# Two tables for a planner that orders an attention and two MLPs on one core

## The chip, the core and the metric

One core of a Trainium2 chip runs the whole program in one launch. TensorE multiplies matrices, VectorE, ScalarE and GpSimd work elementwise, SyncE (SP) issues the transfers. The metric is device microseconds of one execution. The kernel before takes 909.75 us, median of 3 runs (909.4 to 910.39).

## The reference

```python
a = softmax(phi, axis=2)                       # per batch and head, over the sequence
k_m, v_m = einsum('bhsm,bhsd->bhmd', a, k), einsum('bhsm,bhsd->bhmd', a, v)
attn = softmax(q @ k_m.T / sqrt(64)) @ v_m     # 4 batches, 8 heads, 576 tokens, 64 wide, 32 memories
x = attn as (2304, 512)
h = x @ w_in; x = (h * sigmoid(1.702 * h)) @ w_out            # 512 -> 2048 -> 512
xn = x / sqrt(mean(x * x) + 1e-6) * rms_g
out = (silu(xn @ w_gate) * (xn @ w_val)) @ w_out2             # 512 -> 1536 -> 512
```

All inputs are float32; some weights arrive as 64-bit floats, read as pairs of 32-bit words.

## The kernel before, in words

Products run as split pairs: each operand is a rounded part (h) and a remainder (l), and each product is three products, hh, hl and lh. So every converted weight, and every intermediate, needs a rounding copy (mostly ScalarE) and a subtraction for the remainder (sub_lo, GpSimd or VectorE).

The steps are small functions. For each unit u = (batch, group of four heads) the attention goes from ld_phi and ld_src (loads) through att_k1t or att_k1, att_k2 to att_k5 (the memories) and att_q1, att_q3, att_q3s, att_q4 (the queries). The first MLP works on pairs of batches, pr = 0 and 1, and in 8 groups g of 256 hidden columns; vm_part multiplies the values by w_in, a_g1 (pr, g, t) makes gelu for a quarter t of the tokens, a_g2 multiplies by w_out and adds into x2. norm_1 to norm_4 scale. The second MLP is b_g3 (gate, value, their product) and b_g4 (w_out2, added into oacc, and the transfer out), in 6 groups and 6 tiles of 384 tokens. w_load brings half a weight tile, w_conv makes 32-bit floats of it: ScalarE's absolute value, then on VectorE a clamp (tensor_scalar with max and min, lines 549 to 552), a shift and mask, and two bit operations, then a rounding copy and the remainder (line 579). The converted first-MLP weights are written to a cache in DRAM and read back for the second pair.

All of these only record operations. The class Plan then orders them: units (an operation, or a run of products into one PSUM tile) have a duration from `cost` (line 179), a due time from `dues` (line 255), and `order` (line 295) simulates the engines; wherever an engine can start several units within a small slack it takes the one whose due time is earliest. Due times run from the first to the last product and are pulled forward through the predecessors:

```python
u.due = t if u.eng == "PE" and u.line else t + self.LAG
for s in u.then:
    u.due = min(u.due, s.due + s.after[u] - res if u in s.after else s.due)
```

`can` (line 278) says from when a unit's buffers are free: a tag is a ring of slots, and units that aren't urgent leave `spare` slots. `Pulse` (line 39) models TensorE's two clock rates, and `fill` (line 374) puts products of ones_r by itself into the planned gaps of TensorE. `locks` (line 212) keeps VectorE operations with two operands in SBUF, and its fast ones, from overlapping with GpSimd in the plan. At the end `issue` hands every operation to its engine in the planned order (line 403, which is why nearly every instruction of the trace has line 403). Engines work through their queues in that order.

Of the kernel before, what the change touches and what calls it, by code (L numbers as in the profile page):

```python
# [38 lines left out]
class Pulse:  # L39
# [8 lines left out]
    def rate(self, t):  # L48
        k = int(t / self.W)
        if k not in self.slow:  # L50
            j = max(self.slow)
            while j < k:
                share = self.busy.get(j, 0.0) / self.W
                self.slow[j + 1] = share < (0.93 if self.slow[j] else 0.5)
                j += 1
        return 2.0 if self.slow[k] else 1.0

    def took(self, t, occ, dry=False):
        took = left = occ * self.rate(t)
        while not dry and left > 1e-9:  # L60
            k = int(t / self.W)
            part = min(left, (k + 1) * self.W - t + 1e-6)
            self.busy[k] = self.busy.get(k, 0.0) + part
            t, left = t + part, left - part
        return took

# [27 lines left out]
class Tag:  # L94
    def __init__(self, n, strict, spare, ahead):
        self.strict, self.spare, self.ahead = strict, spare, ahead
        self.free, self.queue, self.line, self.next = [0.0] * n, [], [], 0


class Held:  # L100
    def __init__(self, tag, ap):
        self.tag, self.ap, self.users, self.place = tag, ap, [], None


class Unit:
# [11 lines left out]
class Plan:  # L117
# [6 lines left out]
    LAG = 20.0  # L124
    FILL = True

    def __init__(self, nc):
        self.real = dict(zip(self.ENGINES, (nc.gpsimd, nc.tensor, nc.vector, nc.scalar, nc.sync)))
        self.ops, self.tiles, self.seen, self.line, self.keen = [], {}, {}, False, False
        for name in self.ENGINES:  # L130
            setattr(self, name, Queue(self, name))

# [10 lines left out]
        return sum(1 << i for i in range(4) if p0 < 32 * i + 32 and p0 + rows > 32 * i), m  # L143

    def add(self, op):
        self.ops.append(op)
        for x, write in [(x, False) for x in op.ins] + [(op.out, True)]:
            name = x.tensor.name
            held = self.tiles.get(name)
            if held:  # L150
                if x.space == bass.MemoryType.PSUM:

                    q, m, write = 15, 1, True
                else:
                    q, m = self.area(x)
                if held.users:
                    op.behind.append(held.users[0])
                else:
                    op.takes.append(held)
                    held.place = len(held.tag.queue)  # L160
                    held.tag.queue.append(held)
                    held.line, held.rank = op.line, len(held.tag.line)
                    if op.line:
                        held.tag.line.append(held)
                held.users.append(op)
                op.uses.append(held)
            elif name.startswith("cache"):
                q, m = 1, 1 << x.offset // 65536
            else:
                continue  # L170
            past = self.seen.setdefault(name, [])
            op.after += [o for o, oq, om, w in past if (w or write) and oq & q and om & m]
            if write:
                past[:] = [y for y in past if y[1] & ~q or y[2] & ~m]
            past.append((op, q, m, write))


    @staticmethod
    def cost(op):
        def size(x):  # L180
            return reduce(int.__mul__, (n for s, n in x.ap[1:]), 1)

        n = size(op.out)
        if op.eng == "PE":
            if op.name == "transpose":
                return 0.0009 * n, 0.0009 * n + 0.16
            if op.kw["lhsT"].dtype == F32R:
                t = 0.0135 + n / 2400
                return t, t + 0.16
            t = 0.05 if size(op.kw["lhsT"]) == 32 else 0.1 if n > 1 else 0.13  # L190
            return t, t + 0.25
        if op.eng == "ACT":
            return 0.08 + n / 1200, 0.18 + n / 1200
        if op.eng == "POOL":
            two = op.name == "tensor_tensor"
            t = 0.15 + 0.00215 * n if two else 0.05 + 0.00104 * n
            return t, t + 0.05
        if op.eng == "DVE":
            rate = 1920 if Plan.fast(op) else 960
            if op.name == "tensor_reduce":  # L200
                n, rate = size(op.ins[0]), 960 if op.ins[0].ap[-1][0] == 1 else 560
            t = 0.075 + n / rate + (0.04 if n < 20 else 0.0)
            return t, t + 0.08
        return 0.47, 0.0

    @staticmethod
    def fast(op):
# [10 lines left out]
    def units(self):  # L218
# [27 lines left out]
            for p in [*u.after, *u.behind]:  # L246
                p.then.append(u)
        for held in self.tiles.values():
            held.users = list(dict.fromkeys(of[o] for o in held.users))
            held.left = len(held.users)  # L250
        for u in units:
            u.uses = list(dict.fromkeys(h for o in u.ops for h in o.uses))
        return units

    def dues(self, units):

        t = 0.0
        for u in units:
            u.due = t if u.eng == "PE" and u.line else t + self.LAG
            if u.eng == "PE":  # L260
                t += u.occ
        for u in reversed(units):
            dma = 4.0 if u.eng == "SP" else 0.0
            res = u.res + dma + self.SEM
            for s in u.then:
                u.due = min(u.due, s.due + s.after[u] - res if u in s.after else s.due)
            for h in u.uses:
                queue = h.tag.queue if h.tag.strict else h.tag.line
                j = (h.place if h.tag.strict else h.rank) + h.tag.ahead
                if j < len(queue) and (h.tag.strict or h.line):  # L270
                    s = queue[j].users[0]
                    if s.k > u.k:
                        u.due = min(u.due, s.due - res)
            for h in u.takes:
                if h.tag.strict and h.place + 1 < len(h.tag.queue):
                    u.due = min(u.due, h.tag.queue[h.place + 1].users[0].due)

    def can(self, u):

        t = 0.0  # L280
        for h in u.takes:
            tag = h.tag
            if tag.strict and tag.next != h.place:
                return None
            if len(tag.free) <= (0 if u.keen else tag.spare):
                return None
            if u.eng == "PE" and not u.line and any(
                p.start is None and p not in h.users
                for c in h.users if c.eng != "PE" for p in c.after
            ):  # L290
                return None
            t = max(t, sorted(tag.free)[0 if u.keen else tag.spare])
        return t

    def order(self):
        units = self.units()
        self.dues(units)
        free = dict.fromkeys(self.ENGINES, 0.8)
# [6 lines left out]
        while got < len(units):  # L305
# [20 lines left out]
            if best is None:  # L326
                raise RuntimeError(self.stuck(ready))
            t, u = best
            e = u.eng
            ready[e].remove(u)  # L330
            got += 1
            u.bound = (free[e], u.ready, self.can(u), lock if u.locks else 0.0)
            if e == "PE":
                fill = self.fill(u, free[e], t, pulse) if self.FILL else []
                fills += fill
                took = pulse.took(t, u.occ)
                u.start, u.done, free[e] = t, t + took + u.res - u.occ, t + took
            else:
                u.start, u.done, free[e] = t, t + u.res, t + u.occ
# [10 lines left out]
            for h in u.takes:  # L350
                tag = h.tag
                tag.next = max(tag.next, h.place + 1)
                at = max(x for x in tag.free if x <= t + 1e-9)
                tag.free.remove(at)
            for h in u.uses:
                h.left -= 1
                if not h.left:
# [1 line left out]
            for s in u.then:  # L359
                s.wait -= 1  # L360
                if u in s.behind:
                    s.ready = max(s.ready, u.start)
                elif s.eng != e or e == "SP":
                    s.ready = max(s.ready, u.done + self.SEM - s.after[u])
                if not s.wait:
# [8 lines left out]
    def fill(self, u, free, t, pulse):  # L374

        held = next((h for h in u.takes), None)
        if held is None:
            return []
        ops, at, t = [], max([free, min(x for x in held.tag.free)]), t - 0.3
        while True:  # L380
            took = pulse.took(at, 0.0135 + 512 / 2400, dry=True)
            if at + took > t:
# [24 lines left out]
def kernel(  # L407
# [663 lines left out]
    for o in range(4):  # L1071
        nc.vector.memset(maskeo[32 * o : 32 * o + 32, o % 2 : o % 2 + 1], 1.0)

    def line(step, *args):
        plan.line = True
        step(*args)
        plan.line = False

    def do(step):
        plan.keen = step[0] in (norm_1, norm_2, norm_3, norm_4)  # L1080
        step[0](*step[1:])
        plan.keen = False

    def conv(hf):
        w_conv(hf)

    def att_steps(u, k3, k3s, q1, q3s):
        if u[0] < 2:
# [24 lines left out]
            yield from [(norm_4, pr, t, e) for e in range(NE)]  # L1113

    def weights(hf):
        w_load(hf)
        conv(hf)

    def unit(u, k3, q3s):
# [24 lines left out]

    def loads(b):
        for g in range(2):
            ld_phi((b, g))
            ld_src((b, g), 0)
            ld_src((b, g), 1)

    loads(0)
    ins, outs = halves(groups[0])[:2], halves(groups[0])[2:]
    for hf in ins:
        w_load(hf)
    for g in range(2):
        ld_src((0, g), 2)
    for hf in ins:
        conv(hf)
    for g in range(2):
# [4 lines left out]
        line(vm_part, 0, 0, c, 0)  # L1164
    loads(1)
    for g in range(2):
        ld_src((1, g), 2)
    SP.dma_start(out=rg, in_=moe2_rms_g.rearrange("(e p) -> p e", p=P))

    side, per, prev = iter(()), 2, None  # L1170
# [72 lines left out]
```

## Time and profile before

| | us |
|---|---|
| median of 3 runs | 909.75 |
| the profiled execution | 907.28 |
| its span | 905.5 |
| TensorE busy | 887.7 (98%) |
| VectorE busy | 534.4 (59%) |
| ScalarE busy | 412.0 (45%) |
| GpSimd busy | 311.4 (34%) |

The ends of products are modelled in the trace, so a busy TensorE is not one at its peak; products of ones_r count as busy too. Names of tiles come without their number: gr is a_g1's output and its remainder, x is x2, stage the attention's tile, pad and cv the tiles in which weights are converted, a_inh and a_inl a weight's rounded part and remainder. POOL is GpSimd, DVE VectorE, ACT ScalarE, PE TensorE, SPq the queue of SP.

### The profile page before, as it was taken

The numbers are of one execution on the slowest core, as the hardware profiler recorded it, in microseconds if no ns is written. First come the engines' busy times: TensorE is split into PE (matmuls) and PEld (weight loads), VectorE is DVE, ScalarE is ACT, GpSimd is POOL, SyncE is SP. The second block draws the span as 40 slices with busy tenths as digits, with TensorE's granted clock in tenths as the row PEclk, the third lists the DMA queues.
The fourth block names the chain that finished last, engine by engine and source line by source line (L and its number), as shares of the span: only waits on it lengthen the run. The fifth ranks groups of instructions, "written<-read, shape, count | busy, mean of one in ns | idle before, by whom it ended". The sixth has DMA issues, their size and how long they took to land.

```text
span 905.5 us, 15206 instructions
## 1 busy us (share of the span) xinstructions
PE 887.7 (98%) x5916; PEld 841.6 (93%) x5916; DVE 534.4 (59%) x1059; ACT 412.0 (45%) x895; POOL 311.4 (34%) x316
## 2 busy tenths in 40 slices
PE   8999999999999999999999999999999999999997
PEld 6889999888989999999999999999999999999997
DVE  3765888779855355758886574375356337333333
ACT  2665866775757755646656451132132132112110
POOL 1244555544678768775650030021021021001000
PEclk8999999999999999999999999999999999999999
DMA  9961747638321112123332022022003000000124
GB/s 237 243 188 62 195 141 186 176 115 240 97 83 35 49 35 59 54 65 118 93 94 71 1 73 68 1 70 70 1 24 116 1 1 24 1 1 1 51 54 105
DMA packets 40536, 74.64 MB, mean 82 GB/s; under 512 B 3856, under 2 KB 16144, under 8 KB 40464
## 3 DMA queue, kind: packets, MB, share of 16 engines
q1 hardware_dynamic: 40464, 73.68, 29.0%
q8 instruction: 46, 0.75, 0.4%
q14 instruction: 26, 0.21, 0.1%
HBM read 60.56 MB, written 13.11 MB: 81 GB/s over the span
## 4 chain that ended last, share of the span: by engine, by line
PE 81%; DVE 5%; ACT 5%; DMA 4%; POOL 3%; issue 2%; SPq 0%; POOLq 0%; ACTq 0%; DVEq 0%
PE pg L403 74%; DMA raw_a_in<-in_moe_w_in_dram 3%; DVE pad L403 2%; PE pk L403 2%; PE pq L403 2%; PE pvm L403 1%; DMA stage<-in_v_dram 1%; POOL gr L403 1%; ACT L403 1%; ACT pad L403 1%; PE pk4s L403 1%; DVE x L403 1%; ACT gf L403 0%; POOL a_outl L403 0%; DVE stage L403 0%
## 5 line engine op out<-in xcount | busy, mean ns | idle before, releaser
L403 PE MATMUL pg<-gr,a_outh 128*128 128x288 f32 x960 | 204.9, 297 | 0.6 <-POOL gr L403 0.6
L403 PEld LDWEIGHTS pg<-gr,a_outh 128*128 128x128 f32 x960 | 157.7, 188 | 1.5 <-POOL gr L403 1.1
L403 PE MATMUL pg<-gr,a_outl 128*128 128x288 f32 x480 | 141.4, 295 | 0.3 <-POOL a_outl L403 0.3
L403 PE MATMUL pg<-b_o2h,pp 128*128 128x512 f32 x432 | 139.5, 391 | 0.3 <-ACT oacc L403 0.3
L403 POOL TENSOR_TENSOR gr<-gf,gr 128x288 fp32r<-128x288 f32 x128 | 107.8, 856 | 87.4 <-ACT gr L403 69.0
L403 DVE TENSOR_TENSOR x<-x,pg 128x288 f32<-128x288 f32 x224 | 95.8, 447 | 68.3 <-PE pg L403 67.4
L403 DVE TENSOR_TENSOR pf<-sg,pg 128x384 f32<-128x384 f32 x72 | 39.8, 552 | 150.8 <-PE pg L403 131.2
L403 POOL TENSOR_TENSOR b_o2l<-cv,b_o2h 128x512 fp32r<-128x512 f32 x12 | 15.4, 1301 | 267.0 <-ACT b_o2h L403 267.0
L403 ACT ACTIVATE sg<-pg 128x384 f32<-128x384 f32 x72 | 35.4, 492 | 156.7 <-PE pg L403 155.7
L403 PEld LDWEIGHTS pg<-b_o2h,pp 128*128 128x128 f32 x432 | 81.1, 188 | 16.6 <-ACT oacc L403 0.4
L403 ACT CAST pp<-pf 128x384 fp32r<-128x384 f32 x72 | 37.0, 514 | 128.0 <-DVE pf L403 127.5
L403 PEld LDWEIGHTS pg<-gr,a_outl 128*128 128x128 f32 x480 | 90.2, 188 | 0.8 <-POOL a_outl L403 0.5
L403 PE MATMUL pg<-b_o2l,pp 128*128 128x512 f32 x216 | 84.7, 392 | 0.0
L403 DVE TENSOR_TENSOR oacc<-oacc,pg 128x512 f32<-128x512 f32 x90 | 61.5, 684 | 31.4 <-PE pg L403 31.3
L403 ACT ACTIVATE gf<-pg 128x288 f32<-128x288 f32 x128 | 51.1, 409 | 42.3 <-PE pg L403 41.1
L403 ACT CAST gr<-gf 128x288 fp32r<-128x288 f32 x128 | 54.1, 435 | 18.3 <-PE pg L403 11.7
L403 PE MATMUL pg<-xnh,b_gateh 128*128 128x384 f32 x288 | 62.1, 337 | 0.0
L403 PE MATMUL pg<-xnh,b_gatel 128*128 128x384 f32 x288 | 61.8, 335 | 0.0
L403 PE MATMUL pg<-xnh,b_valh 128*128 128x384 f32 x288 | 61.7, 335 | 0.0
L403 PE MATMUL pg<-xnh,b_vall 128*128 128x384 f32 x288 | 61.5, 334 | 0.0
L403 PE MATMUL pg<-xnl,b_valh 128*128 128x384 f32 x288 | 61.5, 334 | 0.0
L403 PE MATMUL pg<-xnl,b_gateh 128*128 128x384 f32 x288 | 61.5, 334 | 0.0
(192 smaller groups left out, 1783.2 us busy)
## 6 DMA issues: line engine op xcount, KB each, us to landing
raw_a_in<-in_moe_w_in_dram SPq DMA_DIRECT2D x16, 512.0 KB, 5.2
raw_a_out<-in_moe_w_out_dram SPq DMA_DIRECT2D x16, 512.0 KB, 4.7
cache<-pad SPq DMA_DIRECT2D x32, 256.0 KB, 4.6
raw_b_gate<-in_moe_w_gate_dram SPq DMA_DIRECT2D x12, 512.0 KB, 3.7
raw_b_val<-in_moe_w_val_dram SPq DMA_DIRECT2D x12, 512.0 KB, 3.6
raw_b_o<-in_moe_w_out_dram SPq DMA_DIRECT2D x12, 512.0 KB, 3.6
stage<-in_k_dram SPq DMA_DIRECT2D x8, 576.0 KB, 7.0
stage<-in_v_dram SPq DMA_DIRECT2D x8, 576.0 KB, 10.5
```

The source lines that it names most:

```text
L403: getattr(self.real[op.eng], op.name)(*op.args, **op.kw)
```

## The change

Every step gets a name, its function and its whole numbers (`at`), and every operation its number within the step. Two tables go by these names. OTHER names operations that go to the other one of VectorE and GpSimd: 98 steps, 122 operations. HASTE names 57 steps whose due time is shifted, 47 earlier (4.6 to 67.8 us) and 10 later (0.9 to 96.5 us). Besides, the planner's costs change (products of the attention longer, PSUM operands longer on ScalarE and VectorE, a gap of 0.03 between dependent VectorE operations), its model of the clock (a lower threshold for slowing down, products of few columns count less), and its slots: a unit takes the slot that was released first.

| operations in OTHER | from | to | number |
|---|---|---|---|
| a_g1, remainder (8 and 17), first pair | GpSimd | VectorE | 26 |
| a_g1, remainder, second pair | GpSimd | VectorE | 20 |
| w_conv a 0, clamp (1) | VectorE | GpSimd | 22 |
| w_conv a 0, remainder (7) | GpSimd | VectorE | 15 |
| w_conv a 1, remainder (1) | GpSimd | VectorE | 11 |
| w_conv b, clamp (1) | VectorE | GpSimd | 4 |
| w_conv b, remainder (6) | GpSimd | VectorE | 4 |
| att_k3, subtraction (2) | GpSimd | VectorE | 2 |
| att_q3s, multiplication (3) | GpSimd | VectorE | 5 |
| norm_1, addition of 768 (2) | GpSimd | VectorE | 3 |
| norm_1, remainder (5) | GpSimd | VectorE | 2 |
| norm_4, remainder (2) | VectorE | GpSimd | 7 |
| b_g3 0 0, remainder (27) | VectorE | GpSimd | 1 |

```diff
-                self.slow[j + 1] = share < (0.93 if self.slow[j] else 0.5)
+                self.slow[j + 1] = share < (0.93 if self.slow[j] else 0.36)
...
-    def took(self, t, occ, dry=False):
+    def took(self, t, occ, streams=1.0, dry=False):
...
-            self.busy[k] = self.busy.get(k, 0.0) + part
+            self.busy[k] = self.busy.get(k, 0.0) + part * streams
...
+    HASTE = {
+        "a_g1 0 2 2": 34.2,
...
+        "b_g4 5 4": -96.5,
+        "ld_src 0 0 1": 46.6,
...
+        "w_conv a 0 4 in 1": 40.2,
+        "w_conv a 0 5 out 0": 41.1,
+        "w_conv a 1 7 in 0": 67.8,
...
+        "w_load a 0 4 out 0": 57.5,
+        "w_load b 0 o2 0": 34.1,
+    }
+
+    OTHER = {
+        "a_g1 0 0 1": (8,),
...
+        "norm_4 0 2 2": (2,),
+        "w_conv a 0 0 in 0": (7,),
+        "w_conv a 0 0 in 1": (1, 7),
...
+    }
...
+        k = self.count[self.step] = self.count.get(self.step, -1) + 1
+        op.step = self.step
+        if k in self.OTHER.get(self.step, ()):
+            op.eng = "POOL" if op.eng == "DVE" else "DVE"
...
-            t = 0.05 if size(op.kw["lhsT"]) == 32 else 0.1 if n > 1 else 0.13
+            t = 0.094 if size(op.kw["lhsT"]) == 32 else 0.17 if n > 1 else 0.22
...
-            return 0.08 + n / 1200, 0.18 + n / 1200
+            t = 0.08 + n / 1200
+            if op.ins[0].space == bass.MemoryType.PSUM:
+                t += 0.13 if op.kw.get("func") is AF.Gelu_apprx_sigmoid else 0.07
+            return t, max(t + 0.04, 0.18 + n / 1200)
...
+            if any(x.space == bass.MemoryType.PSUM for x in op.ins):
+                t += 0.04
...
+        return {1: 0.0, 32: 0.7}.get(op.out.ap[-1][1], 1.0)
...
+            u.due -= self.HASTE.get(u.ops[0].step, 0.0)
...
-            t = max(t, sorted(tag.free)[0 if u.keen else tag.spare])
+            t = max(t, tag.free[0])
...
-                at = max(x for x in tag.free if x <= t + 1e-9)
-                tag.free.remove(at)
+                tag.free.pop(0)
...
+                elif s.eng == e == "DVE":
+                    s.ready = max(s.ready, u.done + 0.03)
...
+    def at(step, *args):
+        said = [a for a in args if isinstance(a, (int, tuple))]
+        plan.step = " ".join([step.__name__, *map(str, said)]).replace("(", "").replace(")", "").replace(",", "").replace("'", "")
...
     def do(step):
+        at(*step)
...
     def conv(hf):
+        at(w_conv, hf)
         w_conv(hf)
```

## Rows read from the trace of the kernel before

**Rows 1.** Stages of the span: busy us of each engine (instructions), PEclk, DMA share, GB/s.

```profile
0.00:44.00 44.00, 41.04 (x303) 34.47 (x304) 24.85 (x70) 17.93 (x44) 10.02 (x19) 0.88 0.97 240
44.00:100.00 56.00, 52.22 (x462) 48.08 (x461) 39.48 (x95) 36.52 (x91) 24.56 (x24) 1.00 0.49 130
100.00:275.00 175.00, 169.98 (x1432) 162.82 (x1431) 138.79 (x292) 117.88 (x273) 99.98 (x102) 1.00 0.54 152
275.00:498.00 223.00, 221.77 (x1598) 218.36 (x1597) 144.20 (x284) 139.99 (x298) 142.17 (x147) 1.00 0.22 68
498.00:905.00 407.00, 402.74 (x2129) 377.92 (x2127) 187.06 (x322) 99.68 (x194) 34.67 (x26) 1.00 0.13 37
```

**Rows 2.** Chain of waits, whole span, in order of time: start us, us, what.

```profile
497.74 403.01 PE pg L403 x2130
...
900.77 0.69 DVE oacc L403
```

**Rows 3.** The same stages, TensorE's products with ones_r alone: stretch, PE busy, PEclk, DMA.

```profile
0.00:44.00 44.00, 22.37 (x76) 0.88 0.97 240
...
44.00:100.00 56.00, 10.09 (x41) 1.00 0.49 130
...
100.00:275.00 175.00, 8.73 (x35) 1.00 0.54 152
```

**Rows 4.** Chain of waits between 35 and 190 us.

```profile
35.98 9.03 DMA stage<-in_v_dram
...
89.83 1.03 DVE stage L403 x2
...
155.47 11.49 DMA raw_a_in<-in_moe_w_in_dram
...
177.54 1.61 DVE pad L403 x4
...
180.08 5.70 DMA raw_a_in<-in_moe_w_in_dram
```

**Rows 5.** Stages again, 200 to 250 us.

```profile
200.00:250.00 50.00, 48.65 (x402) 45.85 (x401) 44.02 (x96) 33.20 (x75) 29.47 (x30) 1.00 0.61 168
```

**Rows 6.** Timeline, 27 to 30 us: start us, us, engine, line, operation, count.

```profile
27.79 1.27 POOL L403 TENSOR_TENSOR a_inl<-pad,a_inh 128x512 fp32r<-128x512 f32 x1 [1.99 <-ACT a_inh L403]
...
27.89 1.72 DVE L403 SCALAR_TENSOR_TENSOR pad<-raw_a_out,pad 128x512 uint32<-128x512 uint32 x1
...
29.80 0.68 DVE L403 SCALAR_TENSOR_TENSOR pad<-raw_a_out,pad 128x512 uint32<-128x512 uint32 x1
```

**Rows 7.** Groups by shape: busy us, mean ns | idle before, who ended it.

```profile
L403 POOL TENSOR_TENSOR gr<-gf,gr 128x288 fp32r<-128x288 f32 x128 | 107.8, 856 | 87.4 <-ACT gr L403 69.0 <-PE pg L403 10.2 <-issue 7.7
...
L403 DVE TENSOR_TENSOR x<-x,pg 128x288 f32<-128x288 f32 x224 | 95.8, 447 | 68.3 <-PE pg L403 67.4
...
L403 DVE TENSOR_TENSOR oacc<-oacc,pg 128x512 f32<-128x512 f32 x90 | 61.5, 684 | 31.4 <-PE pg L403 31.3
...
L403 POOL TENSOR_TENSOR a_inl<-raw_a_in,a_inh 128x512 fp32r<-128x512 f32 x16 | 21.0, 1310 | 1.1
...
L403 DVE TENSOR_SCALAR pad<-pad 128x512 f32<-128x512 f32 x32 | 15.5, 484 | 11.1 <-ACT pad L403 11.1
...
L403 DVE TENSOR_TENSOR xnl<-xnf,xnh 128x384 fp32r<-128x384 f32 x24 | 14.0, 593 | 3.4 <-ACT xnh L403 3.3
...
L403 POOL TENSOR_TENSOR stage<-stage 96x384 f32<-96x384 f32 x16 | 13.0, 829 | 26.7 <-DVE stage L403 21.1 <-ACT stage L403 4.2 <-DVE vm_0l L403 1.1
...
L403 POOL TENSOR_SCALAR a_inh<-raw_a_in 128x512 fp32r<-128x512 f32 x16 | 10.2, 638 | 3.6 <-PE pvm L403 2.9 <-DMA raw_a_in<-cache 0.7
...
L403 DVE TENSOR_TENSOR stage<-pq,stage 96x384 f32<-96x384 f32 x16 | 8.7, 551 | 0.4
...
L403 POOL TENSOR_TENSOR sr<-sq,sr 128x384 fp32r<-128x384 f32 x6 | 6.7, 1110 | 4.1 <-ACT sr L403 4.1
```

**Rows 8.** Timeline at 152 us, SP's queue.

```profile
152.21 0.36 SPq L403 DMA_DIRECT2D stage<-in_k_dram  x1
```

More of the change, by code (lines that the diff above doesn't have):

```diff
@@ L96, in __init__ @@
         self.strict, self.spare, self.ahead = strict, spare, ahead
-        self.free, self.queue, self.line, self.next = [0.0] * n, [], [], 0
+        self.n, self.free, self.queue, self.line, self.next = n, [0.0] * n, [], [], 0
 class Held:
     def __init__(self, tag, ap):
-        self.tag, self.ap, self.users, self.place = tag, ap, [], None
+        self.tag, self.ap, self.ops, self.place = tag, ap, [], None
 class Unit:
@@ L125 @@
     FILL = True
+    HASTE = {
+        "a_g1 0 2 2": 34.2,
+        "a_g1 0 3 0": -35.6,
+        "a_g1 0 6 2": 17.9,
+        "a_g1 1 3 2": 57.3,
+        "a_g1 1 3 3": 40.2,
+        "a_g1 1 6 3": 24.6,
+        "a_g1 1 7 0": 28.0,
+        "a_g1 1 7 2": 17.0,
+        "a_g2 0 0 3": 35.8,
+        "a_g2 0 2 3": -19.2,
+        "a_g2 0 3 1": 7.7,
+        "a_g2 1 0 2": 41.3,
+        "a_g2 1 1 1": 41.2,
+        "att_k1 3 0": 35.9,
+        "att_k3 3 0": 20.5,
+        "att_k4 2 1": 32.9,
+        "att_k4 3 0": 7.4,
+        "att_k5 1 0": 58.0,
+        "att_k5 2 0": -36.4,
+        "att_q1 2 0 0": 22.5,
+        "att_q1 2 1 1": 15.0,
+        "att_q3 2 0 0": 20.7,
+        "att_q3 3 0 0": -0.9,
+        "att_q3 3 1 1": 52.4,
+        "att_q3s 2 1 0": -28.4,
+        "att_q3s 2 1 1": 11.8,
+        "att_q3s 3 0 1": 17.9,
+        "att_q4 1 1 0": 54.2,
+        "att_q4 2 0 1": -9.3,
+        "att_q4 3 0 1": -11.3,
+        "b_g3 0 2": 6.4,
+        "b_g3 1 0": 34.5,
+        "b_g3 1 4": -15.0,
+        "b_g3 1 5": 4.6,
+        "b_g4 5 4": -96.5,
+        "ld_src 0 0 1": 46.6,
+        "norm_2 0 2": 23.2,
+        "norm_3 0 1": 22.5,
+        "norm_4 0 0 2": 28.2,
+        "norm_4 0 1 0": -19.0,
+        "norm_4 0 1 3": 5.2,
+        "norm_4 1 1 1": 26.5,
+        "vm_part 0 1 1 0": 19.0,
+        "vm_part 0 3 0": 18.6,
+        "vm_part 0 3 1": 19.5,
+        "vm_part 0 6 0": 29.2,
+        "vm_part 0 7 0": 37.3,
+        "vm_part 0 7 1": 17.5,
+        "vm_part 1 1 0": 41.6,
+        "vm_part 1 3 1": 50.7,
+        "w_conv a 0 4 in 1": 40.2,
+        "w_conv a 0 5 out 0": 41.1,
+        "w_conv a 1 7 in 0": 67.8,
+        "w_conv b 0 o2 0": 20.1,
+        "w_conv b 0 val 0": 28.6,
+        "w_load a 0 4 out 0": 57.5,
+        "w_load b 0 o2 0": 34.1,
+    }
+    OTHER = {
[98 rows of a table added]
+    }
     def __init__(self, nc):
@@ L129, in __init__ @@
         self.ops, self.tiles, self.seen, self.line, self.keen = [], {}, {}, False, False
+        self.step, self.count = "", {}
         for name in self.ENGINES:
@@ L145, in add @@
     def add(self, op):
+        k = self.count[self.step] = self.count.get(self.step, -1) + 1
+        op.step = self.step
+        if k in self.OTHER.get(self.step, ()):
+            op.eng = "POOL" if op.eng == "DVE" else "DVE"
+        op.key = self.step, k
         self.ops.append(op)
@@ L155, in add @@
                     q, m = self.area(x)
-                if held.users:
-                    op.behind.append(held.users[0])
+                if held.ops:
+                    op.behind.append(held.ops[0])
                 else:
@@ L164, in add @@
                         held.tag.line.append(held)
-                held.users.append(op)
+                held.ops.append(op)
                 op.uses.append(held)
@@ L202, in cost, with streams @@
             t = 0.075 + n / rate + (0.04 if n < 20 else 0.0)
+            if any(x.space == bass.MemoryType.PSUM for x in op.ins):
+                t += 0.04
             return t, t + 0.08
         return 0.47, 0.0
+    @staticmethod
+    def streams(op):
+        return {1: 0.0, 32: 0.7}.get(op.out.ap[-1][1], 1.0)
     @staticmethod
@@ L248, in units @@
         for held in self.tiles.values():
-            held.users = list(dict.fromkeys(of[o] for o in held.users))
+            held.users = list(dict.fromkeys(of[o] for o in held.ops))
             held.left = len(held.users)
+            held.tag.free, held.tag.next = [0.0] * held.tag.n, 0
         for u in units:
@@ L291, in can, with order @@
                 return None
-            t = max(t, sorted(tag.free)[0 if u.keen else tag.spare])
+            t = max(t, tag.free[0])
         return t
-    def order(self):
+    def order(self, until=1e9):
         units = self.units()
@@ L328, in order @@
             t, u = best
+            if t > until:
+                self.planned = units
+                return None
             e = u.eng
@@ L335, in order @@
                 fills += fill
-                took = pulse.took(t, u.occ)
+                took = pulse.took(t, u.occ, self.streams(u.ops[-1]))
                 u.start, u.done, free[e] = t, t + took + u.res - u.occ, t + took
@@ L378, in fill @@
             return []
-        ops, at, t = [], max([free, min(x for x in held.tag.free)]), t - 0.3
+        ops, at, t = [], max(free, held.tag.free[0]), t - 0.3
         while True:
@@ L1072 @@
         nc.vector.memset(maskeo[32 * o : 32 * o + 32, o % 2 : o % 2 + 1], 1.0)
+    def at(step, *args):
+        said = [a for a in args if isinstance(a, (int, tuple))]
+        plan.step = " ".join([step.__name__, *map(str, said)]).replace("(", "").replace(")", "").replace(",", "").replace("'", "")
     def line(step, *args):
+        at(step, *args)
         plan.line = True
@@ L1084, in conv, with load @@
     def conv(hf):
+        at(w_conv, hf)
         w_conv(hf)
+    def load(hf):
+        at(w_load, hf)
+        w_load(hf)
     def att_steps(u, k3, k3s, q1, q3s):
@@ L1115, in weights @@
     def weights(hf):
-        w_load(hf)
+        load(hf)
         conv(hf)
@@ L1146, in loads @@
         for g in range(2):
-            ld_phi((b, g))
-            ld_src((b, g), 0)
-            ld_src((b, g), 1)
+            do((ld_phi, (b, g)))
+            do((ld_src, (b, g), 0))
+            do((ld_src, (b, g), 1))
     loads(0)
@@ L1153 @@
     for hf in ins:
-        w_load(hf)
+        load(hf)
     for g in range(2):
-        ld_src((0, g), 2)
+        do((ld_src, (0, g), 2))
     for hf in ins:
@@ L1166 @@
     for g in range(2):
-        ld_src((1, g), 2)
+        do((ld_src, (1, g), 2))
+    plan.step = "rg"
     SP.dma_start(out=rg, in_=moe2_rms_g.rearrange("(e p) -> p e", p=P))
```

94 rows, old and new, of the table OTHER are left out of this document.

## The prediction

> **What bounds the kernel now.** I read the table of stages first, all engines in five stretches [rows 1]. In the last one, 498 to 905 us, TensorE works 402.7 of 407.0 us, and VectorE needs only 187.1 of them. The chain of waits says the same: one piece of 403.0 us with nothing but matrix products, then an addition and the last transfer [rows 2]. No order of the other engines shortens that, so 44% of the span is out of reach.
>
> What can be gained is TensorE's time that is not a product of the program: its idle time (stretch minus busy, [rows 1]) and the filler products that the plan puts into planned gaps; they multiply ones_r by itself [rows 3]. (In the fourth stretch ones_r is the operand of the norm's products, so none is counted there.)
>
> - 0 to 44 us: idle 3.0, filler 22.4. TensorE waits here for the attention of batch 0. DMA is at 0.97 of its time, so I take this stretch as set by the loads.
> - 44 to 100: idle 3.8, filler 10.1, together 13.9.
> - 100 to 275: idle 5.0, filler 8.7, together 13.7.
> - 275 to 498: idle 1.2, no filler.
>
> From 44 us on, 28.8 us are lost, and that is the most that a better order gives back behind the start. The chain names the losers [rows 4]: in 44 to 100 the load of v for batch 1 (9.03 us on the chain) and then VectorE's softmax; in 100 to 275 the weights, a load that lands after 11.49 us, VectorE's four operations per half weight (one piece of 1.61 us is pad alone), then the next load, 5.70 us. VectorE is the fullest engine behind TensorE: 138.8 of 175 us, and 44.0 of 50 between 200 and 250 [rows 1, 5].
>
> **The shared resource.** At 27.79 GpSimd starts a two-input subtraction of 1.27 us; VectorE's operation on pad that begins at 27.89 takes 1.72 us, while the next of the same kind takes 0.68 alone [rows 6]. An operation of VectorE with two operands in SBUF stands still while GpSimd works. So a GpSimd operation costs VectorE too, and I count both engines and the sum of what they hold, called port time below.
>
> **The table of engines, first pair (slots up to about 290 us).** Durations from [rows 7].
>
> - 26 subtractions of a_g1 (128x288) go from GpSimd, 0.856 us each, to VectorE. With both operands in SBUF this shape isn't in the trace. The same shape with one operand in PSUM takes 0.447; the 384 wide one in SBUF takes 0.593, waits included. I take 0.45, nearest in shape. GpSimd -22.3, VectorE +11.7.
> - 15 subtractions of converted weights (128x512): GpSimd 1.310; VectorE 0.69, by the 512 wide addition (0.684). GpSimd -19.7, VectorE +10.4.
> - 22 clamps of the conversion (tensor_scalar, 128x512) go the other way. VectorE gives 0.484 each, -10.6. On GpSimd the trace shows multiply and add in this shape, 0.638; maximum and minimum it doesn't show, so between 0.638 and the two-input 1.310. I take 0.64: GpSimd +14.1. Each adds a hop to another engine behind ScalarE's absolute value, and queues there behind a subtraction of up to 1.31 us.
> - Attention: five multiplications (0.829 against 0.551) and two subtractions of 768 columns. VectorE's additional column costs (0.684-0.447)/224 = 1.06 ns, so 0.551+0.41 = 0.96; GpSimd takes at least twice its 0.829. VectorE +4.7, GpSimd -7.5.
>
> Sum: VectorE +16.2 us, GpSimd -35.4. Port time: -35.4 + 11.7 + 10.4 + 4.7 - 10.6 = -19.2 us. VectorE gets more work but fewer stops; the two nearly cancel, and what is left is latency: the subtractions that end a_g1 and a weight half, which TensorE waits for, take about half as long.
>
> The Trainium skill speaks against the clamps. Its page "VectorE: DVE Perf Modes", section "Mode 2×_2P — use both read ports for one tensor", says that a float tensor_scalar on SBUF data runs at two elements a cycle on VectorE, by using both read ports. By that rule the move trades VectorE's fastest form for one that blocks it 0.64 us: 22 times 0.16 us worse than the 0.484 it frees, 3.5 us of port time lost. The trace agrees that the form is fast [rows 7]. The sum above already holds these 3.5 us.
>
> **The same table later.** In the second pair (to 498) 20 subtractions of a_g1, 11 of weights, and three additions of 768 and two subtractions of the norm go to VectorE, seven subtractions of norm_4 to GpSimd (0.593 against 1.110): VectorE about +9.0+7.6+2.9+1.1-4.2 = +16.4 on 144.2 of 223 us, 72%. TensorE's 221.8 of 223 hide it; I cost it at nothing. Without cover, the seven would add 7 x 0.52 = 3.6 us. In the last stage four clamps, four subtractions and one subtraction of b_g3 lie beside 402.7 us of TensorE: nothing.
>
> **The table of shifts.** 57 steps, 47 earlier and 10 later. It adds no instruction; it changes who goes first where several units can start, and through the dues of predecessors the loads in front of them. A conversion that goes earlier brings its load, its cache write and its place in SP's, ScalarE's, VectorE's and GpSimd's queues with it, and all that is behind waits for it. Where it can pay: the load of 11.49 us, issued at 155.47, stands behind the next unit's k, v and q, whose issues begin at 152.21 [rows 8]; without them it would land nearer to the 3 to 6 us of the next one on the chain (5.70), some 6 us. w_load and w_conv of groups 4 and 5 are among the shifts. Where it costs: the same 6 us on that unit's attention, hidden while products of earlier groups are left. b_g4 5 4, 96.5 later, moves its four additions and transfers to the end; the number of products is the same, so between 0 and the 0.69 us of one addition [rows 2]; I take 0.
>
> **The planner's costs and slot rule.** These change no instruction either, only its picture: attention's products longer, PSUM reads longer, slots taken in the order of their release. A truer picture puts less on queues that are late on the chip. It has no row; bounds are a loss the size of the idle time it has to plan around (10.0 us from 44 us on) and a gain of the same size; I take it as part of the recovery below.
>
> **The sum.** 44 to 100: half of 13.9, as the loads behind it stay: -7. 100 to 275: the moved ends and the earlier loads lie on the very chain, three quarters of 13.7: -10. 0 to 44, 275 to 905: 0. The profiled execution took 907.28 us (span 905.5), so 890.3; the median is 2.47 above it: **892.8 us**.
>
> **Rivals.**
>
> 1. Everything lost after 44 us comes back: 907.3 - 28.8 + 2.5 = 881. For it: the fillers mark gaps that the plan already saw. Against: batch 1's load of v, 9.03 us on the chain, is needed whatever the order. 0.10.
> 2. The clamps on GpSimd eat the gain: at 1.31 each they add 22 x 0.67 = 14.7 us of port time, or their hop lengthens each conversion by a queueing of 1.3 us. Half of that on the chain takes 7 to 10 us from the 17: 900 to 903. 0.17.
> 3. The loads alone set 44 to 275, and moved work was hidden anyway: 909.8, no change (within 0.2%, 1.8 us, about what a measurement of this kernel can tell). For it: DMA pieces lead the chain in both stretches. Against: VectorE pieces stand between them. 0.07.
> 4. Slower: VectorE becomes the bound. It gets 16.2 us net in the first pair, most of it between 44 and 275 where it works 178.3 of 231 us (77%), which makes 84%; spread evenly, 50 us get 3.5 of it, and the 44.0 of 50 between 200 and 250 [rows 5] become 47.5, or 95%. From 95% on, every softmax and every accumulation queues, PSUM banks come free later, and TensorE follows. Half of the 16.2 shown on TensorE and nothing recovered: 907.3 + 8.1 + 2.5 = 918. Against: its stops behind GpSimd shrink. 0.16.
> 5. The tables do nothing: a key that names no step is silently ignored. The keys match the names that the new labels make (step, then its whole numbers), so I give this no chance of its own; it would come out as rival 3.
>
> **Chances.** The forecast (884 to 899) has 0.50. Faster 0.50+0.10+0.17 = 0.77, same 0.07, slower 0.16. The range reaches from 878 (the first rival's 881, less the 3.0 us of idle time before 44) to 911, which leaves out most of the fourth.
>
> **What would show it.** Right: in 44 to 100 and 100 to 275 fewer fillers and less idle time, by 7 and 10 us; gr's subtractions on VectorE near 0.45; GpSimd's busy time down by about 35 us before 290; the last stage still 403 us, only earlier. Wrong: VectorE over 95% in 150 to 250 with TensorE waiting for x and stage; clamps on GpSimd over 1 us; a granted clock below 1.00 after 44 us where fillers have gone; fresh gaps in the norm's stretch, 275 to 498, which I cost at nothing.

## The result, and the profile after

The changed kernel takes 885.98 us (median of 4 runs, 883.39 to 888.35) against 909.58 of the kernel before (908.51 to 910.39, with a fourth run beside the three of 909.75); the ratio is 0.9741, interval 0.9711 to 0.9771. Forecast were 892.8 us, with a range from 878 to 911. The profiled execution took 885.36 us, span 883.6, which is 21.9 us shorter than before.

The stages of the changed kernel, all engines, columns as in [rows 1]. The edges of the last two are moved to where the unbroken run of products now begins:

```profile
0.00:44.00 44.00, 38.39 (x303) 30.86 (x304) 29.25 (x80) 19.63 (x47) 12.08 (x18) 0.96 1.03 251
44.00:100.00 56.00, 54.56 (x501) 52.38 (x500) 48.20 (x109) 46.52 (x118) 26.97 (x23) 0.97 0.70 186
100.00:275.00 175.00, 168.65 (x1463) 164.01 (x1462) 144.11 (x314) 117.43 (x269) 102.07 (x93) 1.00 0.49 137
275.00:476.00 201.00, 200.87 (x1437) 198.47 (x1437) 147.75 (x296) 127.42 (x269) 104.79 (x105) 1.00 0.23 68
476.00:884.00 408.00, 403.03 (x2130) 377.81 (x2128) 184.18 (x315) 98.43 (x191) 33.72 (x25) 1.00 0.13 38
```

The products with ones_r alone (stretch, PE busy, PEclk, DMA share, GB/s):

```profile
0.00:44.00 44.00, 19.24 (x58) 0.96 1.03 251
44.00:100.00 56.00, 0.68 (x2) 0.97 0.70 186
100.00:275.00 175.00, 0.00 (x0) 1.00 0.49 137
```

The end of the chain of waits:

```profile
484.32 394.72 PE pg L586 x2082
...
879.07 0.69 DVE oacc L586
```

Idle time is the stretch minus PE busy, and filler comes from the second view. From 0 to 44 us the two were 25.3 [rows 1, 3] and are 24.9. From 44 to 100 they were 13.9 and are 2.1 (1.44 + 0.68). From 100 to 275 they were 13.7 and are 6.3, no filler at all. Behind that 1.2 became 0.1. These differences make 20.7 of the 21.9 us. The last stage is what it was: 403.0 us busy in 408 against 402.7 in 407, only some 22 us earlier, and the piece of 394.7 us in the chain answers to the 403.0 of [rows 2].

By the chain [rows 4], what TensorE waited for in 44 to 100 was the attention of batch 1. VectorE's last writes of attnT, batch 0 then batch 1 (timeline; start us, us), before:

```profile
47.08 0.45 DVE L403 TENSOR_TENSOR attnT<-pq,attnT 128x288 fp32r<-128x288 f32 x1
...
96.86 1.19 DVE L403 TENSOR_TENSOR attnT<-pq,attnT 128x288 fp32r<-128x288 f32 x3
```

and after:

```profile
46.69 0.81 DVE L586 TENSOR_TENSOR attnT<-pq,attnT 128x288 fp32r<-128x288 f32 x2
...
83.42 0.82 DVE L586 TENSOR_TENSOR attnT<-pq,attnT 128x288 fp32r<-128x288 f32 x2
```

Batch 0 ends at the same time, 47 us; batch 1 ends at 84.2 instead of 98.1. The loads of its k, v and q are issued from 32.1 to 36.9 us instead of 34.9 to 38.4.

The groups by shape, after (busy us, mean ns | idle before):

```profile
L586 POOL TENSOR_TENSOR gr<-gf,gr 128x288 fp32r<-128x288 f32 x82 | 71.2, 877 | 72.4 <-ACT gr L586 58.2 <-PE pg L586 9.6 <-issue 4.1
...
L586 POOL TENSOR_SCALAR pad<-pad 128x512 f32<-128x512 f32 x22 | 43.0, 1956 | 21.8 <-ACT pad L586 21.6
...
L586 DVE TENSOR_TENSOR gr<-gf,gr 128x288 fp32r<-128x288 f32 x46 | 27.9, 607 | 1.4 <-ACT gr L586 1.0
...
L586 DVE SCALAR_TENSOR_TENSOR pad<-raw_a_in,pad 128x512 uint32<-128x512 uint32 x32 | 21.7, 682 | 0.0
...
L586 POOL TENSOR_SCALAR a_inh<-raw_a_in 128x512 fp32r<-128x512 f32 x16 | 10.5, 668 | 4.7 <-PE pvm L586 2.0 <-PE pg L586 1.6 <-DMA raw_a_in<-cache 1.1
...
L586 DVE TENSOR_TENSOR a_outl<-pad,a_outh 128x512 fp32r<-128x512 f32 x8 | 5.5, 683 | 0.0
```

The 46 moved subtractions of a_g1 take 0.607 on VectorE, stops included, against 0.877 for those left on GpSimd. The clamp is the surprise: 1.956 us on GpSimd, three times the 0.668 of the multiply and add in the same shape, on the same engine, in the same run.

### The profile page after: what moved, and what is told of

It reads as the page before. It is cut to its first block, busy times and chain, and to the rows that moved or that the text cites. A ratio compares the mean times of both kernels' runs of the same rounds, so it can differ in the third digit from the quotient of the medians.

```text
span 883.6 us, 14955 instructions
## 1 busy us (share of the span) xinstructions
PE 865.5 (98%) x5826; PEld 823.5 (93%) x5826; DVE 553.5 (63%) x1113; ACT 409.4 (46%) x891; POOL 279.6 (32%) x262
## 4 chain that ended last, share of the span: by engine, by line
PE 82%; DVE 2%; DMA 1%; ACT 1%; issue 0%; DVEq 0%; SPq 0%
PE pg L586 77%; PE pvm L586 2%; PE pq L586 1%; DMA kmisc<-in_phi_dram 1%; PE pk L586 1%; DVE kmisc L586 0%; PE pnm L586 0%; DVE stage L586 0%; PE pnr L586 0%; DVE gr L586 0%; DVE x L586 0%; DVE vm_7l L586 0%; ACT L586 0%; ACT vm_6h L586 0%; DVE pad L586 0%
## 5 line engine op out<-in xcount | busy, mean ns | idle before, releaser
L586 PE MATMUL pg<-gr,a_outh 128*128 128x288 f32 x960 | 207.0, 297 | 2.8 <-POOL gr L586 1.3
L586 DVE TENSOR_TENSOR x<-x,pg 128x288 f32<-128x288 f32 x224 | 97.8, 449 | 52.4 <-PE pg L586 50.6
L586 POOL TENSOR_TENSOR gr<-gf,gr 128x288 fp32r<-128x288 f32 x82 | 71.2, 877 | 72.4 <-ACT gr L586 58.2
L586 POOL TENSOR_TENSOR b_o2l<-cv,b_o2h 128x512 fp32r<-128x512 f32 x10 | 12.8, 1299 | 253.4 <-ACT b_o2h L586 217.6
```

Source lines behind the costliest of these rows:

```text
L586: getattr(self.real[op.eng], op.name)(*op.args, **op.kw)
```

## The experiments

All ratios are against the kernel before on the same chip (its medians there were 908.1, 905.7 and 907.0 us), so ratios, not microseconds, are compared. Theory A was mine: the engines bring the gain. Theory B: the order does. In e4, e7 and e8 the changed kernel's order of operations is kept; in every other run the planner makes a new one, so its order differs in more than the entries that were edited.

| run | ratio (interval) |
|---|---|
| the change | 0.9741 (0.9711 to 0.9771) |
| e1 new planner, no tables | 0.9934 (0.9909 to 0.9960) |
| e2 OTHER, shifts of the second MLP only | 0.9931 (0.9906 to 0.9956) |
| e3 HASTE alone | 0.9818 (0.9772 to 0.9863) |
| e4 its order, engines of before | 0.9861 (0.9810 to 0.9912) |
| e5 OTHER, five early shifts | 0.9876 (0.9853 to 0.9899) |
| e6 OTHER, all but these five | 0.9885 (0.9844 to 0.9926) |
| e7 its order, clamps back | 0.9736 (0.9706 to 0.9766) |
| e8 its order, what went to VectorE back | 0.9946 (0.9923 to 0.9969) |
| e9 no fillers, planned anew | 0.9944 (0.9919 to 0.9968) |
| e10 shifts dealt out at random | 0.9993 (0.9976 to 1.0010) |
| e11 clamps out of the table, planned anew | 0.9831 (0.9790 to 0.9873) |
| e12 both tables, planner of before | 0.9932 (0.9907 to 0.9958) |

**e1, the planner alone.**

```diff
-    HASTE = { 57 entries }
+    HASTE = {}
-    OTHER = { 98 entries }
+    OTHER = {}
```

> Both tables empty; the planner's new costs, clock model and slot rule stay. Theory A (the engines: halved subtractions and a lighter shared port bring the gain): nothing of it is left, 905 to 912 us. Theory B (the order: it is the truer plan and the shifts that bring the gain): the truer plan has a part of it alone, 896 to 904, with fewer fillers than before (150) and less idle time of TensorE between 44 and 275.

Measured: 901.22 us, 0.9934. The new costs, clock model and slot rule are worth 0.7% by themselves, a quarter of the gain. This fits theory B's range; in favour of A speaks nothing yet. The signs that B named are there: 124 filler products instead of 152 in the three stretches of [rows 3], and between 44 and 275 TensorE is idle for 4.1 us instead of 8.8.

**e2, OTHER alone.**

```diff
+    HASTE = {'b_g3 0 2': 6.4, 'b_g3 1 0': 34.5, 'b_g3 1 4': -15.0, 'b_g3 1 5': 4.6, 'b_g4 5 4': -96.5,
+             'w_conv b 0 o2 0': 20.1, 'w_conv b 0 val 0': 28.6, 'w_load b 0 o2 0': 34.1}
```

> All of OTHER, and of HASTE only the seven shifts of the second MLP and its weights (its stage is full of products, and without them the planner finds no order). Theory A: most of the gain of the whole change, 886 to 894 us, GpSimd's busy time near 280. Theory B: little more than the planner alone gives, 896 to 906.

(The shifts kept are eight, not seven.) Measured: 901.10 us, 0.9931, the same as e1. Moving 122 operations adds nothing to the new planner when no shifts but these eight go with them, although GpSimd's busy time falls to 280.6 us, as theory A had it. Its stages between 44 and 275, and its fillers between 44 and 100:

```profile
44.00:100.00 56.00, 50.65 (x451) 46.38 (x450) 44.80 (x102) 35.97 (x91) 29.64 (x21) 1.00 0.61 170
100.00:275.00 175.00, 166.99 (x1453) 162.78 (x1451) 143.29 (x311) 123.50 (x278) 93.75 (x84) 1.00 0.49 136
```

```profile
44.00:100.00 56.00, 10.42 (x41) 1.00 0.61 170
```

5.4 us idle and 10.4 filler before 100: the loss of the kernel before is all there. Theory A, that the engines bring the gain by themselves, falls here; what they bring in a fitting order is seen in e4 and e8.

**e3, HASTE alone.**

```diff
-    OTHER = { 98 entries }
+    OTHER = {}
```

> All of HASTE, OTHER empty: the engines of before, ordered anew. Theory A: 900 to 910 us, since the shifts were found for other engines and GpSimd still ends every gelu and weight. Theory B: 886 to 896, most of the gain, with VectorE's busy time near the 534 of before.

Measured: 891.23 us, 0.9818, inside theory B's numbers: 1.2% below e1, with VectorE busy for 522.6 us in the profiled execution. Not all of the gain; the rest needs both tables.

**e4, the engines put back in the finished order.** The plan is made with OTHER; an operation is issued on `home`.

```diff
+        op.home = op.eng
         if k in self.OTHER.get(self.step, ()):
             op.eng = "POOL" if op.eng == "DVE" else "DVE"
...
-                getattr(self.real[op.eng], op.name)(*op.args, **op.kw)
+                getattr(self.real[op.home], op.name)(*op.args, **op.kw)
```

> The changed kernel's order of operations, kept as its planner made it, but every operation of OTHER runs on the engine of before, at the same place of the order. Theory A: the gain goes, 900 to 912 us: each late subtraction takes 0.86 or 1.31 us again and VectorE is held at the port. Theory B: the order carries it, 886 to 894.

Measured: 893.80 us, 0.9861, at the upper end of theory B. The order on its own keeps half of the gain, of which the 0.7% of e1 is a part; the engines give 0.9861/0.9741, 1.2%, but only in the order that was made for them.

**e5 and e6, the shifts in two parts.** Theory C: the start decides. Theory D: the values fit only together.

```diff
# e5
-    HASTE = { 57 entries }
+    HASTE = {'ld_src 0 0 1': 46.6, 'att_k5 1 0': 58.0, 'att_q4 1 1 0': 54.2, 'a_g2 0 0 3': 35.8, 'vm_part 0 1 1 0': 19.0,
+             the eight of e2}
# e6: the other 52
```

> OTHER whole; of HASTE only five early steps (v of unit 0 0, att_k5 1 0, att_q4 1 1 0, a_g2 0 0 3, vm_part 0 1 1 0) and the eight of the second MLP. Theory C (the start: batch 1's attention is pulled in front of the first groups' weights, and the whole middle then stands earlier): against the 901.1 of OTHER alone it gives back the most, 887 to 893 us; batch 1's attnT is written by about 84 us instead of 95 to 98. Theory D (57 values fit only together; any part of them is as good as none): 897 to 904.

> OTHER whole; HASTE without those five. Theory C: the stretch to 100 us stays as with OTHER alone (15 us of filler and idle time between 44 and 100), the middle gains some 4 to 8 us: 893 to 898. Theory D: 897 to 904, as the other half.

Measured: 894.05 us, 0.9876, and 893.34 us, 0.9885. e5 lies between the ranges of the two theories, e6 in that of theory C. From e2's 0.9931 each half takes 0.5%, both together 1.9%; the interval of e6 overlaps that of e2, so its share isn't clear of the noise. The stages of e5:

```profile
44.00:100.00 56.00, 54.77 (x501) 52.61 (x502) 48.30 (x109) 46.75 (x117) 26.41 (x23) 0.97 0.73 192
100.00:275.00 175.00, 166.75 (x1428) 162.63 (x1427) 142.72 (x313) 119.79 (x267) 102.47 (x91) 0.98 0.48 134
```

and of e6:

```profile
44.00:100.00 56.00, 52.44 (x454) 48.93 (x453) 42.96 (x102) 38.51 (x96) 27.20 (x22) 0.94 0.63 166
100.00:275.00 175.00, 169.33 (x1469) 165.19 (x1469) 144.89 (x310) 114.86 (x268) 98.87 (x91) 1.00 0.48 138
```

e5's attention of batch 1 ends at 83.8 us, as theory C had it, and 44 to 100 loses only 1.2 us idle (PE busy 54.8 of 56) and 0.7 us of filler. But 100 to 275 gives some of it back: 8.3 us idle, against 6.3 with all shifts, at a granted clock of 0.98. e6 has the better middle (5.7 idle); its attention of batch 1 ends at 96.1 us, and 44 to 100 loses 3.6 us idle and 6.3 of filler, less than the 15 that theory C expected. So the five early shifts bring batch 1's attention forward and with it most of the 44 to 100 gain: theory C's mechanism is seen. Its size isn't; that the head start is kept only when the middle is ordered for it fits these numbers, but isn't shown.

**e7, only the clamps back** (an edit on top of e4's `home`, as is e8's).

```diff
+        if not (op.eng == "POOL" and op.name == "tensor_scalar"):
+            op.home = op.eng
```

> The changed kernel's order kept, only the 26 clamps run on VectorE again (the other entries of OTHER stay). If the clamps on GpSimd cost port time and a hop, as my sum had it (3.5 us): 882 to 886. If they are what makes room on VectorE for the subtractions: 888 to 893, VectorE over 90% between 100 and 275.

Measured: 880.86 us, 0.9736: not to be told from the change's 0.9741. The stage from 100 to 275:

```profile
100.00:275.00 175.00, 171.81 (x1492) 167.81 (x1491) 148.17 (x333) 120.53 (x278) 76.79 (x81) 1.00 0.50 141
```

GpSimd works 76.8 instead of 102.1 us there, VectorE 148.2 instead of 144.1. The clamps on GpSimd made no room that the subtractions needed: 888 us and more would have shown that. Whether they cost something stays open. TensorE is idle for 3.2 us here instead of 6.3, but the two ratios with their intervals leave up to some 4 us either way, so the 3.5 us of the sum are neither shown nor excluded. This is the lowest ratio measured, by less than its uncertainty.

**e8, all that went to VectorE back on GpSimd, clamps left there.**

```diff
+        if not (op.eng == "DVE"):
+            op.home = op.eng
```

> The changed kernel's order kept, everything that went to VectorE (subtractions, multiplications, additions) runs on GpSimd again; the clamps and the eight operations moved off VectorE later stay on GpSimd. If the subtractions' shorter end is the engines' share of the gain: 892 to 900, at or above the 893.8 with all engines back, since GpSimd then has the clamps too. If both moves only count together through the balance of the two engines: the same 890 to 894 as with all back.

Measured: 899.55 us, 0.9946. All of the gain but 0.5% is gone. The stages from 100 to 275 and from 275 to 476, and what TensorE's weight loads waited for over the whole run (us, times, longest):

```profile
100.00:275.00 175.00, 166.77 (x1438) 161.20 (x1438) 137.91 (x280) 116.37 (x264) 136.29 (x126) 1.00 0.49 135
275.00:476.00 201.00, 195.62 (x1405) 191.50 (x1404) 124.60 (x240) 123.52 (x265) 142.45 (x143) 1.00 0.22 63
```

```profile
PEld pg L589 <- POOL gr L589: 12.9, 16, 2.5
...
PEld pvm L589 <- POOL a_inl L589: 3.6, 4, 1.1
```

In the changed kernel the first of these waits is:

```profile
PEld pg L586 <- POOL gr L586: 1.5, 1, 1.5
```

GpSimd works 136.3 of 175 us, and TensorE waits for its gr. More of the loss lies further on: from 275 to 476 TensorE is idle for 5.4 us instead of 0.1, in 100 to 275 for 8.2 instead of 6.3. The run is worse by 0.9% than e4, which has the clamps (and eight later operations) on VectorE: with the subtractions on GpSimd the clamps there, or those eight, do cost; without them (the change against e7) no cost is seen. What the moved subtractions buy, in this order, is that TensorE hardly waits for GpSimd.

**e9, no fillers.**

```diff
-    FILL = True
+    FILL = False
```

> The changed kernel with none of its 60 filler products; all else is its plan. If the fillers only fill time that TensorE has no use for: 884 to 889 us, as with them. If they hold the granted clock up: longer half-rate stretches in the first 60 us (about 7 us of them before), each 3.4 us of half rate costing up to 1.7 us: 889 to 896.

Measured: 901.81 us, 0.9944, more than expected of either. But not all else is the changed kernel's plan, as I had it. The planner's clock model counts the fillers, so without them it makes another order: SyncE's queue differs from its 21st transfer on, VectorE's from its 23rd operation on. The 2% are the price of leaving out the 60 fillers and of this other order together. Stages of e9 (PEclk is the third column from the end):

```profile
20.00:30.00 10.00, 7.95 (x56) 7.64 (x56) 8.51 (x19) 5.50 (x14) 2.34 (x3) 1.00 1.10 248
...
30.00:40.00 10.00, 6.41 (x78) 5.46 (x77) 8.96 (x23) 5.02 (x15) 4.87 (x5) 0.66 0.69 201
...
80.00:100.00 20.00, 14.70 (x103) 13.92 (x104) 15.64 (x38) 12.87 (x35) 8.00 (x7) 0.83 0.70 169
```

A product group of the attention (48 entries, TensorE), the end of batch 0's attention (VectorE) and, in the first and the last line, TensorE's waits where the clock falls, e9:

```profile
33.69 0.42 PE L586 MATMUL pk<-ident,kmisc 96*128 96x96 f32 x1 [3.30 <-DVE kmisc L586]
34.03 2.79 PE L586 MATMUL pk<-stage,e 96*32 96x128 f32 x48
...
57.78 0.46 DVE L586 TENSOR_TENSOR attnT<-pq,attnT 128x288 fp32r<-128x288 f32 x1 [0.39 <-ACT attnT L586]
...
92.30 0.38 PE L586 MATMUL pk4s<-ones_f,kmisc 96*128 96x1 f32 x2 [3.20 <-DVE kmisc L586]
```

and the same group in the changed kernel:

```profile
28.72 1.52 PE L586 MATMUL pk<-stage,e 96*32 96x128 f32 x48
```

At 30 to 40 us, where TensorE had waited 3.30 us for VectorE (tile kmisc), the granted clock is 0.66: part of it at 1.2 instead of 2.4 GHz. The group takes 2.79 us instead of 1.52; batch 0's attention ends at 58.2 instead of 47.5 us. Not all of that is the clock: the group already starts 5.3 us later, behind this wait, and in the changed kernel the product in front of the group isn't at this place. At 80 to 100, with a wait of 3.20 us, the clock falls again (0.83).

The Trainium skill says in "TensorE: Matmul & The Clock Gate", section "HAM oscillation — how this bites in real kernels", that waits between bursts of products put TensorE back to its slow rate, again and again. This run agrees: its clock falls in the two stretches shown, each with a wait of more than 3 us.

What the clock is worth can be read from executions of one and the same kernel: e4's took 898.77 us at a mean granted clock of 0.984 and 888.81 at 0.994, e7's 884.05 at 0.991 and 879.48 at 0.998. That is 0.7 to 1.0 us for each thousandth. e9's seven executions have 0.987 in the mean, the changed kernel's four 0.996. By these prices, as an estimate, the clock makes 6 to 9 of the 18 us or so that e9 loses; the other half isn't explained, and the new order is the nearest candidate. e4's distance to the change holds some of the clock too: its four executions have 0.989 in the mean.

**e10, the same steps, values dealt out at random** (49 of the 57; one deal).

```diff
-        "a_g1 0 2 2": 34.2,
+        "a_g1 0 2 2": another of the 49 values
...
```

> OTHER whole, HASTE with the same 57 steps, but the values of the 49 that are not of the second MLP dealt out among them at random (one deal). Theory C (it is enough that certain steps go earlier, nearly all values being positive): 890 to 896 us, as with the early or the late half. Theory D (the values fit only together, to each other and to the engines): no better than no shifts, 898 to 906.

Measured: 906.21 us, 0.9993. No gain at all, not even the 0.7% of e1. Its start:

```profile
20.00:30.00 10.00, 8.01 (x49) 7.33 (x48) 9.02 (x20) 5.16 (x14) 2.14 (x2) 0.66 1.09 261
30.00:40.00 10.00, 8.68 (x70) 6.68 (x70) 9.07 (x23) 2.44 (x5) 6.01 (x4) 0.50 0.59 182
40.00:50.00 10.00, 9.40 (x54) 9.29 (x55) 6.93 (x18) 6.37 (x21) 1.53 (x2) 0.50 0.97 257
```

Half rate from 30 to 50 us, where the changed kernel had this:

```profile
30.00:40.00 10.00, 9.42 (x80) 7.43 (x69) 9.85 (x29) 6.30 (x20) 5.74 (x5) 1.00 1.09 277
40.00:50.00 10.00, 9.69 (x97) 8.23 (x96) 9.25 (x21) 6.32 (x14) 2.22 (x3) 0.83 1.11 225
```

One deal shows that the steps alone aren't enough; it doesn't show how rare a good deal is.

**e11, clamps out, planned anew; e12, the planner of before.**

```diff
# e11
-        "w_conv a 0 0 in 1": (1, 7),
+        "w_conv a 0 0 in 1": (7,),
... and so for all 26
# e12
-            t = max(t, tag.free[0])
+            t = max(t, sorted(tag.free)[0 if u.keen else tag.spare])
... and the costs, clock model and slots of before
```

> Both tables, but without the 26 clamps, and planned anew, so that the planner no longer counts 0.58 us for an operation of GpSimd that takes 1.96 in the trace. If a plan whose durations are true is worth more than the fit of the tables to it: 876 to 883. Theory D (taking out 26 entries moves the whole plan away from what the shifts were fitted to): 888 to 898.

> Both tables under the costs, clock model and slot rule of before. Theory D: 897 to 905 us, since the tables fit the new costs only; the new planner alone was worth 0.7%, so at or above 893 in any case. If the tables carry their gain into any plan: 889 to 893.

Measured: 892.60 us, 0.9831, and 900.92 us, 0.9932. Both lie in theory D's ranges. The same engines as in e7 under a plan made anew for them are 1% slower than under the old plan. So a new plan alone can move the time by 1%, and differences of that size between two runs that were each planned anew may be the luck of a plan as well as the worth of a table. In e12 the tables bring 0.7% to the planner of before, where they bring 1.9% to the new one: not nothing, but no more than the new planner brings without tables (e1).

## Why the prediction was right or wrong

**The stages: right.** The loss was where [rows 1, 3] put it, and the last stage hid its changes. Of the 28.8 us that I took as the most behind 44 us, some 20 came back. I took 7 of 13.9 us from 44 to 100 and 10 of 13.7 from 100 to 275; measured are 11.8 and 7.4. I had held the first down for the load of v on the chain [rows 4]. That load's two halves are issued 1.9 and 1.8 us earlier than before, and the attention behind them ends 13.8 us earlier, which e5 shows to be the early shifts' work. So my "loads stay, hence half" was the mis-sized term. Neither share, the half and the three quarters, had a row behind it, and their errors have opposite signs: that the forecast came within 7 us is in part luck.

**The engines as cause: wrong as it stood.** The step that failed is the reading of the two tables: the shorter subtractions as the gain, the shifts priced by one load, 6 us each way, and not by whose attention comes first. e2 shows OTHER worth nothing alone, e3 HASTE worth 1.2% on top of e1. The subtractions and the few operations that went to VectorE with them do have their share, but in the finished order only: 1.3% with the clamps on VectorE (e4 against e7), 2% with the clamps on GpSimd (e8 against the change).

**The later table: put at nothing, wrongly.** I let TensorE's 221.8 of 223 us hide the second pair's moved subtractions. With what went to VectorE back on GpSimd, e8, TensorE is idle for 5.4 us between 275 and 476 instead of 0.1.

**Durations.** A moved gr that meets no GpSimd operation takes 0.451 (23 of them in the trace), as my 0.45; with stops 0.607. The 512 wide subtraction took 0.683, as my 0.69. In the mean the moved gr gained less than I had it, 0.607 against 0.877 on GpSimd and not half. The clamp at 1.956 lies beyond my upper bound of 1.310: I bounded it by the operations that GpSimd's rows showed, and a kind that they didn't show was slower than all of them. The 22 alone are 43.0 us instead of 14.1. So GpSimd's busy time up to 275 us didn't fall by 35 us: it was 134.6 [rows 1] and is 141.1, by then some 20 us further on in the program.

**The port: half right.** Two-input operations of GpSimd hold VectorE up as in [rows 6]. The clamps hardly do. Timeline of the changed kernel (start us, us):

```profile
101.62 4.21 POOL L586 TENSOR_SCALAR pad<-pad 128x512 f32<-128x512 f32 x2 [0.88 <-ACT pad L586]
...
103.31 0.45 DVE L586 TENSOR_TENSOR gr<-gf,gr 128x288 fp32r<-128x288 f32 x1
...
104.05 0.77 DVE L586 TENSOR_SCALAR pad<-pad 128x512 uint32<-128x512 uint32 x1
```

Two clamps run from 101.6 to 105.8, and a two-operand subtraction of VectorE takes 0.45 in between, its time alone. Of VectorE's 160 SCALAR_TENSOR_TENSOR operations (136 bit operations of the weights, 24 of the norm), 13 met mostly a clamp and took 0.693 in the mean, 113 met nothing and took 0.675, and 34 met mostly a two-input operation of GpSimd and took 0.877. What a clamp does hold up here is VectorE's fast form: the shift and mask in the last line takes 0.77 instead of the 0.42 that it takes alone, and the three of this run that met nothing but a clamp took 0.77 to 0.82. So GpSimd's busy time isn't port time by itself. My second rival took it as such; at half as much again as the 1.31 us that it feared for a clamp, the 7 to 10 us that it put on the chain didn't come (e7 leaves room for some 4).

**The slower rival: not seen.** VectorE's share from 44 to 275 went from 178.3 to 192.3 us of 231, 83%, and 48.2 of 56 in 44 to 100, with TensorE idle 1.4. In 150 to 250, where I had feared 95%, it worked 91.1 of 100 us and TensorE 97.9. A VectorE as full as that was no bound in this order.

**The clock: named as a danger, and rightly.** After 44 us it fell below 1.00 once (0.83 from 40 to 50 us), without undoing the gain. But I had counted the fillers as lost time and nothing else. e9 shows a lower clock without them and a run 2% longer; what of that is the fillers' own worth, and what the other order's, isn't shown.

**Left open.** 1.2 us of the 21.9 are in no stretch's idle time or filler. The granted clock is a candidate: 0.88 over the first 44 us before, against 0.96 and then 0.97 to 100 us after, which makes 5.3 and 3.4 us of full clock lost, 1.8 in favour (an estimate from the stages' means). How the early and the late shifts carry each other isn't taken apart. Nor is e9: the finished order issued without its fillers was not run.

## What to carry to other kernels

A plan for in-order queues is worth as much as the engines it names: test a table of placements and a table of orders each alone and together before crediting either, because here, beyond the new planner, the placements alone gave nothing, the shifts alone 1.2%, and both 1.9%. Test a placement in the finished order too (e4, e7, e8), since a plan made anew moved the time by 1% by itself (e11). Bound an operation on another engine by its own kind, or leave the bound open. Before striking out products that compute nothing, look at what the clock does in the gap that they leave, and keep the order when you try it.

## What the runs showed of the hardware that was not expected

- On GpSimd tensor_scalar with maximum and minimum took 1.956 us for 128x512 floats, with multiply and add 0.668 (same run, the group rows above), and VectorE's two-operand operations went on beside the former (0.693 against 0.675 us alone), while its shift and mask took 0.77 to 0.82 instead of 0.42.
- Executions of one kernel differ in their mean granted clock, and in time with it: e4's from 888.81 us at 0.994 to 898.77 at 0.984.
- An 886 us program planned and run without its 60 filler products, 58 of them in the first 44 us, took 2% longer (e9); fillers and order are not separated there.
